# Attention rows scaled when they are written, or when they are gathered

## The chip, the cores and the metric

One core of a Trainium2 chip runs the kernel. The metric is device time in microseconds (us) of one launch, the lower the better. Inputs and outputs are float32 in device memory; a row of 512 floats is 2 KB.

## What is computed

Linear attention with a normalisation, followed by a mixture of eight experts of which each token uses one. Cut to what matters:

```python
kv  = einsum('bhsd,bhse->bhde', k, v)              # 8 batches, 8 heads, 576 tokens, 64 wide
out = einsum('bhsd,bhde->bhse', q, kv)
rms = sqrt(mean(out*out, -1) + 1e-6)               # one number per token and head
x   = (out / rms * g_norm) as [4608 tokens, 512]
logits = x @ w_gate;  e = argmax(logits)           # 8 experts
gate_w = softmax(logits)[e]
eom    = sigmoid(x @ w_output_gate)
y[token] = gate_w * eom[e] * (relu(x @ w1[e]) @ w2[e])
```

Each token thus has eight factors 1/rms (one per head) and one factor gate_w * eom[e], which is called its scale here. The scale is positive, so it may be applied to x in front of the relu or to the result behind w2.

## The kernel before

**First phase.** 4608 tokens are 36 tiles of 128 rows. Eight batches are read in order; for each, `kv_step` (L472) makes kv out of four loads of 512 KB and a remainder, `kvT_part` and `m_part` prepare the products with the gates, and `out_tile` (L540) makes the rows of the tiles whose batches are ready: four or five tiles per batch, one batch behind the loads. ScalarE copies each tile to `xrow` and squares it (`out_rows`), VectorE sums the squares (`sums`, L587).

**Routing.** `route` (L599) is a generator that handles a group of 8, 8, 8, 7 and 5 tiles in eight steps. Step 1 makes `rv` = 1/rms with nine small VectorE instructions (L608 to L622); 2 and 3 make the logits and the one-hot of the expert (`ohb`); 4 counts rows on TensorE (`mrp`, L665 to L672); 5 is two exponentials; 6 makes the scale, multiplies it into `rv` (L701), has GpSimd multiply each tile of the group by `rv` (L710, one instruction per tile, in place) and sends the rows to `xs` in device memory; 7 makes one 128x128 bfloat16 mark matrix per tile (`la`, L720) and the columns `rrc` (L723 to L726); 8 multiplies marks and columns on TensorE (L729) and adds the product to the index table `tsum`. Step 8 of the third group gives the rows of the first run, the lead run: the first 384 tokens of the most frequent expert among the first 24 tiles.

**Order.** PE (TensorE), ACT (ScalarE), DVE (VectorE) and POOL (GpSimd) run their instructions in the order written: a table `STEPS` says after which tile each step of a group is issued, and the string `TAIL` orders what comes behind the last tile. In `TAIL` a digit is the next step of that group, `Q` empties the pending copies and sums, `G` gathers the lead run's rows (`gather(0)`), sets `mark` on POOL (transfers ordered behind the gather wait for it) and opens the late row writes; `W` loads the lead expert's w2; `C` is twelve matmuls of ones into `mrp`; `L` is the next step of the lead run (split of the first w1 block into a high and a low part, three transposed stages, second split, eight `mm1`), and `S` a split of w2. SP (SyncE) issues the plain transfers in program order, each when its semaphores allow.

**Second phase.** Nine runs follow (the lead run, the rest of its expert, seven experts). Per run `mm1` makes eight blocks of h (three matmuls where full precision takes one, since operands are split in two parts; L308), `mm2` makes y tile by tile (L350, L356). During `mm1` of a run the next run's rows are gathered by POOL (L246) as buffers come free; during `mm2` they are transposed (`stage`, L270) and split (L275, L276). `wlo` (L224, L231) is the DVE half of a weight split. y is copied out of PSUM by ACT (L365) and scattered by POOL (L366). A loop behind the runs handles experts with more rows than their capacity; it is not entered in the profile.

The lines around the change, as they stand before:

```python
for j in range(k):                                              # step 6
    xv = x[:, j].rearrange("q (p u d) -> q u p d", p=NP, u=2)
    f = rv[:, c0 + j - g0].rearrange(...).unsqueeze(3).to_broadcast([P, 2, NP, D])
    nc.gpsimd.tensor_tensor(out=xv, in0=xv, in1=f, op=ALU.mult)
xwrite(c0, xs[...], x)
```

## Time and profile before

| | us |
|---|---|
| median of 3 runs | 626.33 |
| lowest, highest | 624.49, 630.56 |
| profiled execution: its time | 623.01 |
| profiled execution: span | 620.9 |
| last tile of the first phase ends on PE | about 124.3 |
| first `mm1` matmul | 158.9 |
| last y tile's matmuls end | about 603.7 |

The profile is of one execution. Busy times overlap between engines; a wait names the engine and line that ended it. PEclk is the clock that TensorE was granted, as a share of 2.4 GHz; 0.5 is its lower level, 1.2 GHz. Times within the span count from its start.

### The profile page before, as it was taken

To read this page: it belongs to the slowest core of one execution; us is meant where nothing else is said; L and a number is where in the kernel's file an instruction comes from. 1 tells how busy PE (TensorE), PEld (TensorE's weight loads), DVE (VectorE), ACT (ScalarE), POOL (GpSimd) and SP (SyncE) were. 2 spreads that over 40 slices of the span, in tenths; PEclk is the share of its full clock that TensorE was granted. 3 is DMA by queue.
4 is the path that set the end of the run, shared out by engine and by line. 5 is a ranking of instruction groups with operands and counts; after the bars stand their busy time and mean duration, and the time that the engine had idled before them with its cause. 6 is when DMAs were issued, how large, how long until landed. Compare 5 with 4: busy or idle time off the path is not lost.

```text
span 620.9 us, 10566 instructions
## 1 busy us (share of the span) xinstructions
PE 571.0 (92%) x4253; PEld 505.7 (81%) x4253; DVE 284.1 (46%) x569; ACT 217.5 (35%) x405; POOL 123.2 (20%) x128
## 2 busy tenths in 40 slices
PE   7895959906899999999999999999999999999995
PEld 5785849804898989988988998799889879988974
DVE  2159698998641445632452144234314523532410
ACT  1364443500632433431343234233414433432310
POOL 1005054163052040041013103200510221011011
PEclk8798675555899999999999999999999999999998
DMA  8999971419246372343233524343343334210001
GB/s 267 357 407 406 408 274 65 142 31 358 69 144 228 113 222 68 104 131 136 70 130 102 167 69 136 120 138 97 116 145 102 109 109 163 69 52 19 1 17 44
DMA packets 28739, 91.64 MB, mean 148 GB/s; under 512 B 4081, under 2 KB 4209, under 8 KB 28688
## 3 DMA queue, kind: packets, MB, share of 16 engines
q1 hardware_dynamic: 21952, 71.33, 32.5%
q0 software_dynamic: 6304, 19.39, 9.9%
q8 instruction: 35, 0.57, 0.4%
q10 hardware_dynamic: 432, 0.21, 0.1%
q14 instruction: 16, 0.13, 0.1%
HBM read 72.03 MB, written 19.41 MB: 147 GB/s over the span
## 4 chain that ended last, share of the span: by engine, by line
PE 80%; DVE 11%; DMA 5%; issue 2%; ACT 1%; POOL 0%; POOLq 0%; ACTq 0%; DVEq 0%
PE hps L308 35%; PE yps L356 31%; PE ops L561 4%; DMA ld<-kvm 3%; DVE la L720 3%; PE yps L350 3%; PE tps L270 3%; PE kvp L487 2%; DMA gcol<-gn 1%; DVE ss L587 1%; PE kvp L503 1%; DVE gp L629 0%; DMA out<-y,oidx 0%; PE mrp L470 0%; ACT sq L577 0%
## 5 line engine op out<-in xcount | busy, mean ns | idle before, releaser
L356 PE MATMUL yps<-whi,hT 128*128 128x512 f32 (+3 forms) x592 | 195.1, 398 | 0.0
L308 PE MATMUL hps<-xT,whi 128*128 128x256 f32 (+8 forms) x1024 | 189.9, 303 | 2.0 <-ACT xT L275 2.0
L308 PEld LDWEIGHTS hps<-xT,whi 128*128 128x128 f32 x1024 | 158.4, 189 | 3.4 <-ACT xT L275 2.2
L356 PEld LDWEIGHTS yps<-whi,hT 128*128 128x128 f32 (+3 forms) x592 | 110.1, 186 | 24.2
L308 PE MATMUL hps<-xT,wlo 128*128 128x304 f32 (+8 forms) x512 | 118.3, 302 | 0.0
L324 DVE SCALAR_TENSOR_TENSOR hT<-hps,hT 128x512 fp32r<-128x512 f32 (+6 forms) x112 | 58.1, 519 | 130.4 <-ACT hT L323 130.4
L356 PE MATMUL yps<-wlo,hT 128*128 128x512 f32 (+3 forms) x296 | 115.9, 392 | 0.0
L323 ACT ACTIVATE hT<-hps 128x512 fp32r<-128x512 f32 (+6 forms) x112 | 51.5, 460 | 141.5 <-PE hps L308 108.6
L308 PEld LDWEIGHTS hps<-xT,wlo 128*128 128x128 f32 x512 | 86.5, 189 | 0.0
L366 POOL DMA_INDIRECT out<-y,oidx x42 | 42.1, 1003 | 215.7 <-ACT y L365 188.9
L246 POOL DMA_INDIRECT xg<-xs,gidx x42 | 41.9, 998 | 169.2 <-PE tps L270 130.3
L356 PEld LDWEIGHTS yps<-wlo,hT 128*128 128x128 f32 (+3 forms) x296 | 55.1, 186 | 11.3
L224 DVE SCALAR_TENSOR_TENSOR wlo<-wraw,gcol,whi 128x1024 fp32r<-128x1024 f32 x32 | 41.1, 1283 | 40.1 <-ACT whi L221 40.0
L710 POOL TENSOR_TENSOR xrow<-xrow,rv 128x512 f32<-128x512 f32 x36 | 36.3, 1044 | 103.6 <-DVE rv L701 64.9
L275 ACT CAST xT<-tps 128x512 fp32r<-128x512 f32 (+9 forms) x45 | 23.1, 518 | 85.0 <-PE tps L270 83.2
L561 PE MATMUL ops<-aug,ld 64*128 64x80 f32 (+1 forms) x640 | 52.5, 331 | 0.0
L276 DVE TENSOR_TENSOR xT<-tps,xT 128x512 fp32r<-128x512 f32 (+9 forms) x45 | 27.1, 606 | 54.8 <-ACT xT L275 50.2
L561 PEld LDWEIGHTS ops<-aug,ld 64*128 64x128 f32 (+1 forms) x640 | 46.4, 232 | 4.0 <-issue 1.8
L365 ACT COPY y<-yps 128x512 f32<-128x512 f32 (+3 forms) x37 | 21.7, 586 | 71.9 <-PE yps L356 68.2
L231 DVE TENSOR_TENSOR wlo<-wraw,whi 128x1024 fp32r<-128x1024 f32 x32 | 39.2, 1225 | 13.7 <-ACT whi L228 8.8
L587 DVE TENSOR_REDUCE ss<-sq 128x8 f32<-128x512 f32 x36 | 24.2, 681 | 30.5 <-ACT sq L577 30.4
L487 PE MATMUL kvp<-ld 128*64 128x64 f32 (+1 forms) x640 | 33.3, 266 | 4.8 <-DMA ld<-kvm 4.5
(155 smaller groups left out, 429.3 us busy)
## 6 DMA issues: line engine op xcount, KB each, us to landing
wraw<-w SPq DMA_DIRECT2D x64, 512.0 KB, 3.4
ld<-kvm SPq DMA_DIRECT2D x32, 512.0 KB, 10.1
ld<-qT SPq DMA_DIRECT2D x18, 512.0 KB, 10.2
xs<-xrow SPq DMA_DIRECT2D x9, 512.0 KB, 4.5
xs<-xrow SPq DMA_DIRECT2D x2, 1280.0 KB, 6.4
xs<-xrow SPq DMA_DIRECT2D x1, 2048.0 KB, 15.3
ld<-rem SPq DMA_DIRECT2D x3, 512.0 KB, 10.1
xg<-xs,gidx POOLq DMA_INDIRECT x42
```

The costliest lines, as they stand in the source:

```text
L224: eng.scalar_tensor_tensor(out=lo, in0=r, scalar=gcol[:, 0:1], in1=hi.bitcast(F32), op0=ALU.mult, op1=ALU.subtract)
L231: eng.tensor_tensor(out=lo, in0=r, in1=hi.bitcast(F32), op=ALU.subtract)
L246: gathered = nc.gpsimd.indirect_dma_start(out=x[:M, :], out_offset=None, in_=rows, in_offset=bass.IndirectOffsetOnAxis(ap=gidx[:M, p, t:t ...
L308: nc.tensor.matmul(ps[:, j, :n], w[:, o:o + P], x[d][:, j * N:j * N + n], start=(d == 0 and k == 0), stop=(d == 3 and k == 2))
L323: nc.scalar.activation(hh, x, AF.Relu)
L324: nc.vector.scalar_tensor_tensor(out=v(h[:, l:l + n]), in0=x, scalar=0.0, in1=hh.bitcast(F32), op0=ALU.max, op1=ALU.subtract)
L356: nc.tensor.matmul(ps[:M], a, b, start=(f == 0 and k == 0), stop=(f == 7 and k == 2))
L366: i_ = nc.gpsimd.indirect_dma_start(out=out, out_offset=bass.IndirectOffsetOnAxis(ap=oidx[:M, p, t:t + 1], axis=0), in_=y[:M], in_offset=N ...
L487: nc.tensor.matmul(ps[u * D:(u + 1) * D, p * D:(p + 1) * D], k, v, start=(s == 0 and p == 0), stop=(s == 4 and p == NP - 1))
L561: nc.tensor.matmul(v[r0:r0 + m, u, p, :], qt[g // 2][r, p, q0:q0 + m], augs[b % 3][r, p, :], start=True, stop=True)
L587: nc.vector.tensor_reduce(out=o, in_=sq, axis=AX.X, op=ALU.add)
L710: nc.gpsimd.tensor_tensor(out=xv, in0=xv, in1=f, op=ALU.mult)
```

## The change

The rows are written to `xs` without any multiplication. A row becomes 528 floats wide (`XW`): 512 values, then the eight factors 1/rms, then the scale, then seven floats of nothing (set to zero at the start). Step 1 of `route` has POOL copy `rv` into the tail of each row buffer (12 small copies in all), step 6 has DVE write the scale there; the multiply by L701 and the 36 POOL multiplies of L710 are gone. Behind each gather, POOL now multiplies the gathered tile by the eight factors of its rows (`scale_heads`, one instruction per gathered tile: 3 in the lead run, 39 in the others); DVE copies the scale to `tl` when the tile is staged; and the scale is applied when y leaves PSUM: as the `scale` of ACT's copy, or, for the five half tiles, with one more DVE instruction. The marks `la` read the float32 tile `ni` where they read a bfloat16 copy of it; they stay bfloat16. `TAIL` is another string: steps 7 and 8 of the fourth group and 2 to 5 of the last stand ahead of the first weight split, two `C` instead of one stand between the last group's steps 4 and 6, the three stages stand ahead of its step 8, and `W` stands behind the second split.

```diff
-TAIL = "Q3G4L434344C4C4C4WCLLLLLLSLSLSLSLLL"
+TAIL = "Q3G4343C44C4CL44CLLL4LWLSLSLSLSLLLL"
...
+NORMS = "PPP"
...
-            x = take([P, DM], F32, "xg")
+            x = take([P, XW], F32, "xg")
...
+    def scale_heads(x, eng):
+        v = x[:, 0:DM].rearrange("p (h d) -> p h d", d=D)
+        f = x[:, C_RMS:C_RMS + H].unsqueeze(2).to_broadcast([x.shape[0], H, D])
+        eng.tensor_tensor(out=v, in0=v, in1=f, op=ALU.mult)
+
+    def scale_rows(i):
+        for k, (t, c0, M) in enumerate(tiles_of(i)):
+            if i == 0 and NORMS[k] == "V":
+                continue
+            scale_heads(xg[(RUNS[i][0], t)][:M], nc.gpsimd)
...
+        tl = cst.tile([P, 1], F32, name="tl", bufs=14)
+        nc.vector.tensor_copy(tl[:M], x[:M, C_SCALE:C_SCALE + 1])
+        tails[(p, t)] = tl
...
+            nc.vector.tensor_scalar(out=y[:M], in0=y[:M], scalar1=tl[:M, 0:1], scalar2=None, op0=ALU.mult)
         else:
-            nc.scalar.copy(y[:M], ps[:M])
+            nc.scalar.activation(y[:M], ps[:M], AF.Copy, scale=tl[:M, 0:1])
...
+        for c0, k, x in chunks_of(gi):
+            nc.gpsimd.tensor_copy(x[:, :, C_RMS:C_RMS + H].rearrange("q t (p u) -> q t u p", u=2),
+                                  rv[:, c0 - g0:c0 - g0 + k].rearrange("q t (u p) -> q t u p", u=2))
...
-        vec.tensor_tensor(out=se[:, :n], in0=se[:, :n], in1=eo[:, :n], op=ALU.mult)
-        vec.tensor_tensor(out=rv, in0=rv, in1=se[:, :n].unsqueeze(2).to_broadcast([P, n, E]), op=ALU.mult)
...
-            for j in range(k):
-                xv = x[:, j].rearrange("q (p u d) -> q u p d", p=NP, u=2)
-                f = rv[:, c0 + j - g0].rearrange("q (u p) -> q u p", u=2).unsqueeze(3).to_broadcast([P, 2, NP, D])
-                nc.gpsimd.tensor_tensor(out=xv, in0=xv, in1=f, op=ALU.mult)
+            t = c0 - g0
+            vec.tensor_tensor(out=x[:, :, C_SCALE], in0=se[:, t:t + k], in1=eo[:, t:t + k], op=ALU.mult)
...
-            vec.tensor_scalar(out=la, in0=nib, scalar1=lon[:, t:t + 1], scalar2=None, op0=ALU.is_equal)
+            vec.tensor_scalar(out=la, in0=ni, scalar1=lon[:, t:t + 1], scalar2=None, op0=ALU.is_equal)
...
             gather(0)
+            scale_rows(0)
             behind.append(nc.gpsimd.memset(mark, 0.0))
...
                 gather(1)
+                scale_rows(1)
...
+                    if f == 3 and not last_run:
+                        scale_rows(i + 1)
```

What this moves, at three places. Names as above; `xg` is a gathered tile, `gp` the logits of a group, `hps` the sums of `mm1`.

POOL, from the first group's rows to the first gather of the second phase, before:

```order
L418 CAST gfull<-cf 128x1728
L710 ISA
L710 TENSOR_TENSOR xrow_125<-xrow_125,rv 128x2x4x64 x8
L710 TENSOR_TENSOR xrow<-xrow,rv 128x2x4x64 x23
L246 DMA xg<-xs,gidx 128x512 x3
L815 MEMSET mark 128x1
L710 TENSOR_TENSOR xrow<-xrow,rv 128x2x4x64 x5
L246 DMA xg<-xs,gidx 128x512 x3
```

and now:

```order
L441 CAST gfull<-cf 128x1728
L646 COPY xrow_123<-rv 128x8x2x4
L646 COPY xrow<-rv 128x2x2x4 x9
L646 COPY xrow<-rv 128x5x2x4
L251 DMA xg<-xs,gidx 128x528 x3
L267 ISA
L267 TENSOR_TENSOR xg<-xg 128x512 x3
L837 MEMSET mark 128x1
L646 COPY xrow<-rv 128x5x2x4
L251 DMA xg<-xs,gidx 128x528 x2
L267 TENSOR_TENSOR xg<-xg 128x512
L251 DMA xg<-xs,gidx 128x528
```

The lead run's gather stood behind 31 multiplies and now stands behind 11 copies; the three multiplies of its tiles stand ahead of `mark` and of the last group's copy.

DVE, from the last group's `rv` (step 1) on, before:

```order
L622 SCALAR_TENSOR_TENSOR rv<-ru,ry 128x40
L223 TENSOR_SCALAR whi<-wraw,gcol 128x1024
L224 SCALAR_TENSOR_TENSOR wlo<-wraw,gcol,whi 128x1024
L629 TENSOR_TENSOR gp<-gp,rv 128x5x64 x2
L720 TENSOR_SCALAR la<-nib,rlon 128x128 x7
L723 TENSOR_TENSOR rrc<-cf,rhk 128x7x48
L725 TENSOR_TENSOR rrc<-rrc,gfull 128x7x48
L726 TENSOR_SCALAR rrc<-rrc,cf 128x7x48
```

and now, a little later in the same stretch (the split's new place):

```order
L658 TENSOR_REDUCE lg<-gp 128x5x8
L703 TENSOR_TENSOR rog<-ohb_119,lg 128x40
L705 TENSOR_REDUCE rogs<-rog 128x5
L706 TENSOR_SCALAR rogs<-rogs 128x5
L228 TENSOR_SCALAR whi<-wraw,gcol 128x1024
L229 SCALAR_TENSOR_TENSOR wlo<-wraw,gcol,whi 128x1024
L713 TENSOR_TENSOR rw<-mrp,ohb_119 128x40
L715 TENSOR_REDUCE slots<-rw 128x5
```

The split of the first w1 block moved from behind step 1 of the last group to just ahead of its step 6 (`rw`).

DVE, up to the split of the lead run's transposed rows (`xT`, six instructions), before:

```order
L906 TENSOR_TENSOR t_142<-tbl,perm 128x336
L874 SCALAR_TENSOR_TENSOR gl<-t_2042 128x6
L908 TENSOR_REDUCE gif<-t_142 128x42
L887 COPY gif<-gl 128x3
L909 CAST gidx<-gif 128x42
L888 CAST gidx<-gif 128x3
L879 TENSOR_SCALAR zf<-gif 128x3
L879 TENSOR_SCALAR zf<-gif 128x42
L880 SCALAR_TENSOR_TENSOR oidx<-gif,zf 128x3
L880 SCALAR_TENSOR_TENSOR oidx<-gif,zf 128x42
L276 TENSOR_TENSOR xT<-tps,xT 128x2x128 x6
```

and now:

```order
L924 TENSOR_TENSOR t_149<-perm,cf 128x56
L297 TENSOR_TENSOR xT<-tps,xT 128x2x128
L925 TENSOR_REDUCE eposf<-t_149 128x7
L926 CAST epos<-eposf 128x7
L297 TENSOR_TENSOR xT<-tps,xT 128x2x128
L287 COPY tl<-xg 128x1
L297 TENSOR_TENSOR xT<-tps,xT 128x2x128 x2
L287 COPY tl<-xg 128x1
L297 TENSOR_TENSOR xT<-tps,xT 128x2x128 x2
L754 TENSOR_TENSOR tsum<-mrp,tsum 128x96
```

The index table's work from `tsum` to `oidx` stood ahead of the six `xT` and now stands behind them.


## Rows read from the trace of the kernel before

**Rows 1.** Stretches of the execution: busy time of PE, of its weight loads, of DVE, ACT and POOL, with counts in brackets; then the granted clock, the share of the DMA engines and GB/s.

```profile
60.00:70.00 10.00, 8.68 (x93) 7.68 (x93) 9.12 (x26) 4.50 (x11) 0.06 (x1) 0.50 1.03 408
70.00:80.00 10.00, 10.00 (x191) 9.06 (x189) 4.22 (x20) 5.20 (x16) 0.00 (x0) 0.80 1.03 405
90.00:100.00 10.00, 10.00 (x118) 8.78 (x116) 8.56 (x27) 3.33 (x10) 0.00 (x0) 0.50 0.08 29
250.00:300.00 50.00, 50.00 (x271) 43.72 (x271) 20.21 (x33) 17.20 (x25) 11.03 (x11) 1.00 0.36 121
```

**Rows 2.** PE in order of time in the first phase: start, time, line, operands, count, and in brackets the idle time before and what ended it. L487 at 39.59, 48.03, 65.48 and 77.58 begins the third, fourth, fifth and sixth batch (counted from 0).

```profile
39.59 0.69 PE L487 MATMUL kvp<-ld 128*64 128x64 f32 x16
...
48.03 0.67 PE L487 MATMUL kvp<-ld 128*64 128x64 f32 x16
...
61.32 0.80 PE L729 MATMUL mrp<-rrc,la 128*128 128x96 bf16 x8 [6.31 <-DVE rrc L726]
...
65.48 1.10 PE L487 MATMUL kvp<-ld 128*64 128x64 f32 x16
...
77.58 0.66 PE L487 MATMUL kvp<-ld 128*64 128x64 f32 x16
...
89.60 0.80 PE L729 MATMUL mrp<-rrc,la 128*128 128x96 bf16 x8 [7.12 <-DVE rrc L726]
...
97.34 0.24 PE L665 MATMUL mrp<-erow,row 128*128 128x72 bf16 x1
```

**Rows 3.** The marks on DVE in order of time: start, time of all, line, count (the first group's, the fourth's, the last's).

```profile
52.38 7.74 DVE L720 TENSOR_SCALAR la<-nib,rlon 128x128 bf16<-128x128 bf16 x8
...
137.76 1.41 DVE L720 TENSOR_SCALAR la<-nib,rlon 128x128 bf16<-128x128 bf16 x7
...
146.45 4.24 DVE L720 TENSOR_SCALAR la<-nib,rlon 128x128 bf16<-128x128 bf16 x5
```

**Rows 4.** POOL's multiplies of rows in order of time (the first group's and the fourth's).

```profile
52.02 8.04 POOL L710 TENSOR_TENSOR xrow<-xrow,rv 128x512 f32<-128x512 f32 x8 [44.60 <-DVE rv L701]
...
127.89 7.07 POOL L710 TENSOR_TENSOR xrow<-xrow,rv 128x512 f32<-128x512 f32 x7 [17.34 <-DVE ra L608]
```

**Rows 5.** Other DVE instructions in order of time: one of the start that takes float32 and a column per partition and gives bfloat16, as the new marks do; the first and the last of the second group's steps 1 to 4 (62.33, 71.45); three sums ahead of the third group's steps 1 to 3 (89.47) and the end of those (97.29).

```profile
7.68 0.28 DVE L425 TENSOR_SCALAR triu<-cf,m 128x128 bf16<-128x128 f32 x1
...
62.33 0.68 DVE L587 TENSOR_REDUCE ss<-sq 128x8 f32<-128x512 f32 x1
...
71.45 0.17 DVE L681 TENSOR_SCALAR rogs<-rogs 128x8 f32<-128x8 f32 x1
...
89.47 1.86 DVE L587 TENSOR_REDUCE ss<-sq 128x8 f32<-128x512 f32 x3
...
97.29 0.23 DVE L652 TENSOR_TENSOR ohb<-rsc,rsx 128x64 bf16<-128x64 f32 x1
```

**Rows 6.** DVE behind the last tile, in order of time: step 6 of the fourth group (126.02); the seven instructions L616 to L622 of step 1 of the last group, first and last (128.10, 134.12); its step 6 (144.78); the index table (153.87 up to the next row); the first `xT`.

```profile
126.02 0.21 DVE L688 TENSOR_TENSOR rw<-mrp,ohb 128x56 f32<-128x56 f32 x1
...
128.10 0.92 DVE L616 SCALAR_TENSOR_TENSOR ru<-ry 128x40 f32<-128x40 f32 x1
...
134.12 0.90 DVE L622 SCALAR_TENSOR_TENSOR rv<-ru,ry 128x40 f32<-128x40 f32 x1
...
144.78 0.20 DVE L688 TENSOR_TENSOR rw<-mrp,ohb 128x40 f32<-128x40 f32 x1 [2.01 <-PE mrp L470]
...
153.87 0.25 DVE L733 TENSOR_TENSOR tsum<-mrp,tsum 128x96 f32<-128x96 f32 x1
...
156.57 0.42 DVE L276 TENSOR_TENSOR xT<-tps,xT 128x256 fp32r<-128x256 f32 x1
```

**Rows 7.** PE in order of time: the matmuls of ones between the phases (12, then 24), the first `mm1` matmuls, and the transposes of the second tile of the run behind the lead run.

```profile
142.01 2.73 PE L470 MATMUL mrp<-ones 128*128 128x256 bf16 x12
146.59 5.28 PE L470 MATMUL mrp<-ones 128*128 128x256 bf16 x24 [1.84 <-DVE cnt L705]
...
158.92 1.20 PE L308 MATMUL hps<-xT,whi 128*128 128x384 f32 x2 [1.96 <-ACT xT L275]
...
182.12 0.60 PE L270 MATMUL tps<-ident,xg 128*128 128x128 f32 x4
```

**Rows 8.** The second phase: POOL's first gather for the run behind the lead run, and its last gather for a later run (order of time); from the chain of work that ended last, the start of that later run's transposes, and the last y tile's scatter from issue to landing.

```profile
173.65 1.72 POOL L246 DMA_INDIRECT xg<-xs,gidx  x1 [22.00 <-PE hps L308]
...
333.95 0.91 POOL L246 DMA_INDIRECT xg<-xs,gidx  x1 [0.58 <-PE tps L270]
...
375.56 0.44 PE tps L270 x4
...
604.55 2.73 DMA out<-y,oidx
```

**Rows 9.** Groups of like instructions: count, busy us, mean ns of one, idle time before: the DVE half of w1's split, and ACT's copy of 1024 columns with a scale (L221) and without (L228).

```profile
L224 DVE SCALAR_TENSOR_TENSOR wlo<-wraw,gcol,whi 128x1024 fp32r<-128x1024 f32 x32 | 41.1, 1283 | 40.1 <-ACT whi L221 40.0
...
L221 ACT ACTIVATE whi<-wraw,gcol 128x1024 fp32r<-128x1024 f32 x31 | 35.7, 1153 | 0.0
L228 ACT CAST whi<-wraw 128x1024 fp32r<-128x1024 f32 x32 | 33.3, 1041 | 0.0
```

**Rows 10.** The last loads of the first phase: SP's last issue of them (start, time, count), and the page's row of these loads (size, median time from issue to landing).

```profile
68.96 1.61 SPq L463 DMA_DIRECT2D ld<-qT  x2
...
ld<-qT SPq DMA_DIRECT2D x18, 512.0 KB, 10.2
```

More of the change, by code (lines that the diff above doesn't have):

```diff
@@ L29 @@
 NT = NTOK // P
+XW = DM + 16
 W = D + 2 * E
+C_RMS = DM
+C_SCALE = DM + H
 CAP = [692, 656, 632, 608, 592, 572, 560, 544]
@@ L237, in drop @@
             give(w)
-    xg, xT, hT = {}, {}, {}
+    xg, tails, xT, hT = {}, {}, {}, {}
     def gather(i):
@@ L262, in stage @@
         x = xg.pop((p, t))
+        if i == 0 and NORMS[k] == "V":
+            scale_heads(x[:M], nc.vector)
         if k == 0:
@@ L340, in mm2 @@
         ny += 1
+        tl = tails.pop((p, t))
         for f in range(8):
@@ L409, in body @@
                                 scalar1=gcol[r, 0:1], scalar2=None, op0=ALU.mult)
-    zrow = c1.tile([P, 4], F32, name="zrow")
+    zrow = c1.tile([XW // 16, 16], F32, name="zrow")
     nc.gpsimd.memset(zrow, 0.0)
-    nc.gpsimd.dma_start(out=xs[0:1, :].rearrange("o (a x) -> (o a) x", x=4), in_=zrow)
+    nc.gpsimd.dma_start(out=xs[0:1, :].rearrange("o (a x) -> (o a) x", x=16), in_=zrow)
     erow = c1.tile([P, E], BF16, name="erow")
@@ L421, in body @@
     tsum = c1.tile([P, 2, E * TMAX], F32, name="tsum")
-    nib = c1.tile([P, P], BF16, name="nib")
-    nc.vector.tensor_copy(nib, ni)
     triu = c1.tile([P, P], BF16, name="triu")
@@ L528, in body @@
             k = NT - sum(BIG.values()) - 2 * ROWS
-            x = c1.tile([P, k, DM], F32, name="xrow0")
+            x = c1.tile([P, k, XW], F32, name="xrow0")
         elif g in BIG:
             k = BIG[g]
-            x = mem.tile([P, k, DM], F32, name="xrow", tag=f"xT{list(BIG).index(g)}")
+            x = mem.tile([P, k, XW], F32, name="xrow", tag=f"xT{list(BIG).index(g)}")
         else:
             k = 2
-            x = take([P, k, DM], F32, "xrow")
+            x = take([P, k, XW], F32, "xrow")
         chunks.append((g, k, x))
+        nc.gpsimd.memset(x[:, :, C_SCALE:XW], 0.0)
         g += k
@@ L574, in out_rows @@
         v = ps[:, :, 0:NP * W].rearrange("q u (p y) -> q u p y", p=NP)
-        nc.scalar.copy(xrow.rearrange("q (p u d) -> q u p d", p=NP, u=2), v[:, :, :, 0:D])
+        nc.scalar.copy(xrow[:, 0:DM].rearrange("q (p u d) -> q u p d", p=NP, u=2), v[:, :, :, 0:D])
         sq = wk.tile([P, H, D], F32, name="sq", bufs=4)
@@ L1069, in body @@
                     ws.append(t)
-            x = so.tile([P, DM], F32, name="ox")
+            x = so.tile([P, XW], F32, name="ox")
             nc.gpsimd.indirect_dma_start(out=x, out_offset=None, in_=xs,
                                          in_offset=bass.IndirectOffsetOnAxis(ap=gi[:, 0:1], axis=0))
+            scale_heads(x, nc.gpsimd)
             ps = pt.tile([P, 4, P], F32, name="ops")
@@ L1089, in body @@
             y = so.tile([P, DM], F32, name="oy")
-            nc.scalar.copy(y, py)
+            nc.scalar.activation(y, py, AF.Copy, scale=x[:, C_SCALE:C_SCALE + 1])
             nc.gpsimd.indirect_dma_start(out=out, out_offset=bass.IndirectOffsetOnAxis(ap=oi[:, 0:1], axis=0),
@@ L1109, in build @@
     out = nc.dram_tensor("out", (NTOK, DM), F32, kind="ExternalOutput").ap()
-    xs = nc.dram_tensor("xs", (NTOK + 1, DM), F32).ap()
+    xs = nc.dram_tensor("xs", (NTOK + 1, XW), F32).ap()
     tab = nc.dram_tensor("tab", (P, NOVER), F32).ap()
```

## The prediction

> **What bounds the kernel now.** I read the stretches first, then PE in order of time, then the engines that PE waits for.
>
> From 158.92 on PE is never short of work: busy 50.00 of 50 us at full clock in a stretch like 250 to 300, with DVE at 20.2 and ACT at 17.2 [rows 1], and the transfers hidden. What comes before 158.92 can be shortened; what comes after is 462.0 us of the 620.9 and moves only if it is disturbed.
>
> In the first phase PE stands twice for the same thing: 6.31 us before 61.32 and 7.12 us before 89.60, both until DVE has the columns `rrc` of step 7 [rows 2]. In front of `rrc` stand the marks: 7.74 us for eight, about 0.96 each, where the fourth group's seven took 1.41 us, 0.20 each [rows 3]. Those of 0.96 ran beside POOL's multiplies (52.02 to 60.06, about 1.0 each), those of 0.20 after the fourth group's had ended at 134.96 [rows 4]. So each mark waited for one POOL instruction. It is the same with the seven small instructions 128.10 to 134.12: about 1.0 us apart, again beside seven multiplies [rows 4, 6].
>
> Each stop costs twice: the clock is 0.50 in 60 to 70, behind the first stop, and still 0.50 in 90 to 100 with PE busy throughout, behind the second [rows 1].
>
> The Trainium skill ("SBUF — State Buffer", section "SBUF: two separate sides") says that DVE and GpSimd share one pair of ports, held exclusively for a whole instruction, and that a DVE instruction in a two-port mode, or one with two inputs from SBUF, has to wait. The trace agrees: 0.96 us against 0.20.
>
> **Term 1, the first phase: 17.8 us less.** The multiplies leave this phase; what POOL gets is 12 copies of 16 to 64 columns, at most one marks' pitch (0.20) each for DVE and off PE's path. The new marks read float32. The nearest row is `triu`, float32 to bfloat16 with a column operand, 0.28 us [rows 5]; bounds 0.20 and 0.28 a mark; I take 0.20, the pitch, so eight take 1.6.
>
> - First stop: the marks end at 54.0, `rrc` adds 1.3, PE goes on at 55.3 and not at 61.32: 6.0. It has then waited about 0.3 us, and I keep its clock. The piece to the fifth batch took 4.2 us at half clock (61.32 to 65.48); at full some 2.5, which sets the batch's start to 57.8.
> - Fifth batch: the third, of as many tiles, took 8.4 us at full clock (39.59 to 48.03 [rows 2]); with 0.3 for the matmuls of step 4 it ends at 66.5, not at 77.58.
> - Sixth batch up to the second group's marks: 4.9 us (77.58 to the stop, 89.60 less 7.12 [rows 2]), so PE asks for `rrc` at 71.4. DVE: steps 1 to 4 with their sums take 9.3 us without a pause (62.33 to 71.6 [rows 5]); from 56.0 that is 65.3. Then three sums and step 6, 3.5 together, marks 1.6, `rrc` 1.2: 71.6. Both arrive together, and PE goes on at 71.8, not at 89.60: **17.8**.
> - Behind this DVE is late. From 89.47 to the end of the one-hot at 97.52 it took 8.05 us without a multiply beside it [rows 5]: now 71.7 to 79.8. PE at full clock needs about 4.3 us for what it took 7.7 for at half clock (89.60 to 97.34 [rows 2]), is there at 76.1, and stands 3.7 us.
>
> That stand decides the size. Stops of 6.3 and 7.1 took the clock away, and behind the second it did not return while the phase lasted. I take it that 3.7 us does the same. From 79.8 on all then runs as it ran from 97.5: PE at half clock, DVE level with it, 17.8 us earlier to the end. DVE's step 6 of the fourth group starts at S = 108.2 instead of 126.02.
>
> **Term 2, from S to the first `mm1`: 8.5 us less.** It took 158.92 - 126.02 = 32.9. Now, from S, by DVE's own pieces without a multiply beside them: step 6 of the fourth group 1.65, step 1 of the last 2.2 (it took 7.3 with the seven held ones [rows 6]), marks and columns 2.15, steps 2 and 3 2.6, step 4 1.1: S + 9.7. The first split (2.0) stands here now: S + 11.7. Step 6 of the last group waits for ones, as at 144.78 [rows 6], but for two `C` behind step 4 instead of one. PE starts the first `C` at S + 7.2 (2.7 us), counts rows, and needs 5.3 us for 24 ones at half clock [rows 7]: S + 15.7. Step 6 1.7, five marks 1.0 (they took 4.2 [rows 3]), columns and the expert order 2.6: first `xT` at S + 20.7. The index table's 2.7 us (153.87 to 156.57 [rows 6]) now stands behind the `xT`. From the first `xT` to `mm1` it took 2.35; three `tl` copies add about 0.4. `mm1` starts at S + 23.4: 9.5 less. If the ones warm PE earlier, 24 cost 1.5 to 2 us less.
>
> Against that I set 1.0 us. The lead run's gather no longer waits behind 31 multiplies, and its three tiles are multiplied shortly before S, beside DVE's two-input instructions of the fourth group. Bounds: 0, and 3.1 (all three multiplies). The rows are ready some 15 us ahead of their transposes.
>
> **Term 3, the second phase: 0.5 us more.** POOL gets 39 multiplies of about 1.0 us. For late runs they have cover: the last gather of a run is issued at 333.95, its transposes begin at 375.56 [rows 8]. Not so for the run behind the lead run: its first gather is issued 14.7 us after `mm1` starts (173.65), its second tile transposed at 23.2 (182.12 [rows 7, 8]). In these 8.5 us POOL now has four gathers (1.72, and three of 0.91 with a gap of 0.3: 5.4 in all), two multiplies (2.1) and what is left of the first tile's landing (2.7 from issue to landing, as the last scatter's [rows 8], so up to 1.7): 7.5 to 9.2. Bounds 0 and 2 us late; I take 0.5. DVE's extra work (42 copies `tl`, five short multiplies of half tiles) falls where DVE is 40% busy; without that cover it would be some 9 us at the marks' 0.20 each. ACT's copy with a scale costs 0.11 us more per 1024 columns [rows 9]; only the last one lies on the path. w2's loads move behind the last row write on SP; they land 1 to 3 us ahead of their splits by my count, bounds 0 and 3 us lost.
>
> **Sum.** 623.0 (the profiled execution's time, 2.1 over its span) - 17.8 - 8.5 + 0.5 = 597.2. The median shown, 626.33, lies 3.3 above that execution, its lowest run 1.5. **I predict 597 us.**
>
> **Rivals.**
>
> *The clock survives the 3.7 us.* Then DVE is the bound from 79.8: seventh batch with step 6, marks and table of the third group to 90.6, then sums and steps 1 to 6 of the fourth, S near 102 instead of 108.2: **591**. For it: PE is dense around that stand, and 70 to 80 shows 0.80 after a stop [rows 1], so the clock does come back in this phase. Against: behind the second stop it did not.
>
> *The clock falls at the first, short wait and stays low.* Then only the two stops go, 13.1 us, and the work that ran at full clock between them (in 70 to 80, and up to 82.5; some 8 us) takes about 7 longer: 6 us instead of 17.8, **609**. Against: a wait of 0.3 us is short.
>
> *The marks take long of themselves*, and the change to float32 doesn't shorten them: then the stops stay and only the seven small instructions and the order of the tail are gained, about 5 us: **618**. Against: 0.20 each without POOL [rows 3].
>
> *Slower: the multiplies bite in the loop.* By the port rule each of the 39 can hold a DVE weight split of 1.28 us, one of two inputs from SBUF [rows 9], or be held by it, and DVE's later halves of h wait behind. On POOL a multiply that waits for its gather to land stands in front of the scatters and of the next gather. It decides once rows or splits arrive later than PE's slack. If each multiply cost PE its full 1.04 us, 40.6 us come back: **638**. Against: 42 us of cover for a later run, DVE at 40%. For: the cover of the run behind the lead run is about used up. The Trainium skill's rule, named above, allows this; by it alone the sum would go up by no more than these 40.6.
>
> *Loads as the bound of the first phase*: the last are issued by 70.6 and land near 80.8 [rows 10]; the last batch's products and five tiles need some 7 us more, about 88 in all. S at 102 or 108 lies behind that, so I give this no chance of its own.
>
> **How the numbers follow.** Forecast 0.50, clock kept 0.28, clock low early 0.13, long marks 0.05, slower 0.04. The forecast's own range is 592 to 604: the collisions (0 to 3), the next run's rows (0 to 2), w2 (0 to 3), warm ones (-2), and the 1.5 to 3.3 us by which the shown runs lie above the profiled one. To hold 8 in 10 the range takes in the kept clock and the early low one: 586 to 612. One per cent, 6.3 us, is about what can be told from no change. Below 620 lie the first three and part of the fourth: faster 0.93, same 0.03, slower 0.04.
>
> **What would show it.** The profile of the changed kernel should have marks of 0.2 to 0.28 us each in all groups; no wait of PE for `rrc` over 1 us; one wait of 3 to 4 us for `ohb` near 76 to 80; the clock at 0.50 behind it (if at 1.00, the first rival); step 6 of the fourth group near 108; 23 to 25 us from there to `mm1`; `mm1` starting near 132; and from there 462 to 464 us to the end. If that last stretch has grown by more than 3 us, the fourth rival is at work; if PE still stands 6 us at marks, the third. I am wrong in kind if DVE or POOL is what PE waits for in the second phase.

## The result, and the profile after

The changed kernel takes **596.42 us** in the median (589.71 to 596.93, 4 runs) beside 625.64 of the kernel before: ratio 0.949, 95% interval 0.941 to 0.958. The profiled execution took 596.93 us, its span is 595.1. Executions over 1.5% slower than the fastest of their kernel (up to 1426 us, with matmuls about twice as long in that one) are left out of the ratios, but two of the profiles below, of "before, no multiplies" and of "30 + 90 ones", are of such executions.

All comparisons below use four marks of an execution. T is the start of the fourth batch (batches are counted from 0, as in the prediction), ahead of the first group's marks; S is DVE's step 6 of the fourth group; M is the first `mm1` matmul; the end is that of the span. T differs from one execution to the next, without the change (47.65 to 51.69, and 61.64 once) as with it (45.69 to 51.79).

| profiled execution of | T | T to S | S to M | M to end | span |
|---|---|---|---|---|---|
| before | 48.03 | 78.0 | 32.9 | 462.0 | 620.9 |
| the change | 51.73 | 60.3 | 21.0 | 462.0 | 595.1 |

PE of the changed kernel in order of time (start, time, line, operands, count, in brackets the idle time before and what ended it):

```profile
51.73 0.67 PE L508 MATMUL kvp<-ld 128*64 128x64 f32 x16
...
58.75 0.50 PE L750 MATMUL mrp<-rrc,la 128*128 128x96 bf16 x8
61.07 0.66 PE L508 MATMUL kvp<-ld 128*64 128x64 f32 x16
...
75.35 0.50 PE L750 MATMUL mrp<-rrc,la 128*128 128x96 bf16 x8 [1.00 <-DVE rrc L747]
...
83.31 0.35 PE L695 MATMUL mrp<-ohb,ones 128*128 128x64 bf16 x8 [3.37 <-DVE ohb L677]
...
84.96 2.00 PE L583 MATMUL ops<-aug,ld 64*128 64x80 f32 x16
...
122.32 3.99 PE L491 MATMUL mrp<-ones 128*128 128x256 bf16 x24
...
133.08 1.02 PE L329 MATMUL hps<-xT,whi 128*128 128x384 f32 x2 [2.42 <-ACT xT L296]
```

The two stops of 6.31 and 7.12 us [rows 2] are gone: no wait at 58.75, 1.00 us before 75.35. The one stand left is the 3.37 us for the one-hot; behind it a tile's sixteen matmuls take 2.00 us, where they took 1.12 ahead of it. DVE shows why the stops went, and the collision near S (same columns):

```profile
55.88 1.65 DVE L741 TENSOR_SCALAR la<-ni,rlon 128x128 bf16<-128x128 f32 x8
...
72.55 1.65 DVE L741 TENSOR_SCALAR la<-ni,rlon 128x128 bf16<-128x128 f32 x8
...
109.33 0.87 DVE L706 TENSOR_SCALAR rogs<-rogs 128x7 f32<-128x7 f32 x1
110.12 2.02 DVE L609 TENSOR_REDUCE ss<-sq 128x8 f32<-128x512 f32 x3
112.06 0.21 DVE L713 TENSOR_TENSOR rw<-mrp,ohb 128x56 f32<-128x56 f32 x1
...
112.55 0.55 DVE L717 TENSOR_SCALAR rhk<-slots 128x7 f32<-128x7 f32 x1
```

Eight marks take 1.65 us instead of 7.74 [rows 3]. Beside POOL's three multiplies for the lead run `rogs` and `rhk` are stretched (0.87 and 0.55; both take 0.17 elsewhere). The stretches of the changed kernel (busy time of PE, its loads, DVE, ACT, POOL; then the granted clock, DMA share, GB/s):

```profile
10.00:20.00 10.00, 7.79 (x85) 5.11 (x81) 0.50 (x2) 0.96 (x3) 0.00 (x0) 0.61 1.03 350
20.00:30.00 10.00, 10.00 (x116) 9.21 (x118) 1.37 (x2) 3.02 (x7) 0.00 (x0) 0.50 1.02 393
30.00:40.00 10.00, 10.00 (x172) 8.87 (x170) 2.74 (x4) 5.87 (x14) 0.00 (x0) 0.70 1.03 418
...
80.00:90.00 10.00, 6.70 (x83) 6.12 (x84) 8.93 (x39) 3.39 (x11) 1.18 (x4) 0.69 0.69 250
90.00:100.00 10.00, 9.56 (x112) 8.38 (x113) 4.01 (x16) 3.62 (x10) 0.00 (x0) 0.50 0.88 310
100.00:110.00 10.00, 9.20 (x104) 8.49 (x102) 9.17 (x29) 6.69 (x16) 4.51 (x6) 0.50 0.23 59
```

and of the kernel before, for the start:

```profile
10.00:20.00 10.00, 7.85 (x109) 5.43 (x107) 0.50 (x2) 0.96 (x3) 0.00 (x0) 0.84 1.04 336
20.00:30.00 10.00, 9.76 (x140) 8.72 (x137) 1.52 (x3) 4.55 (x13) 0.00 (x0) 0.69 1.01 345
30.00:40.00 10.00, 9.35 (x206) 8.38 (x208) 3.60 (x6) 7.47 (x21) 0.00 (x0) 1.00 1.03 408
```

The clock of the first 40 us differs from execution to execution (0.84, 0.69, 1.00 before; 0.61, 0.50, 0.70 here). From 20 to 40 PE is never idle here, so this clock is what makes T 3.7 us later. Behind the 3.37 us stand it is 0.69 in 80 to 90 and 0.50 from 90 to 110.

In the second phase PE's waits are 0.3 us for a multiply, once, and the start of `mm1` itself (waiting engine and line, what ended it: us in total, times, longest):

```profile
PE hps L329 <- ACT xT L296: 2.4, 1, 2.4
PE tps L291 <- POOL xg L267: 0.3, 1, 0.3
```

That M to end is 462.0 in both does not mean that nothing changed in it. In the first 5 us of `mm1` the granted clock is 1.00 here and was 0.66 before, so the transposes of the run behind the lead run begin 19.4 us behind M instead of 20.7. From there to the end it takes 442.6 us instead of 441.3. PE, before (one row) and now (its second tile shows the wait):

```profile
179.60 0.60 PE L270 MATMUL tps<-ident,xg 128*128 128x128 f32 x4
```

```profile
152.47 0.60 PE L291 MATMUL tps<-ident,xg 128*128 128x128 f32 x4
...
155.50 0.66 PE L291 MATMUL tps<-ident,xg 128*128 128x128 f32 x4 [0.35 <-POOL xg L267]
```

### The profile page after: what moved, and what is told of

Read it like the earlier page. It is cut to its first block, busy times and chain, and to the rows that moved or that the text cites. A ratio compares the mean times of both kernels' runs of the same rounds, so it can differ in the third digit from the quotient of the medians.

```text
span 595.1 us, 10650 instructions
## 1 busy us (share of the span) xinstructions
PE 564.3 (95%) x4253; PEld 499.8 (84%) x4253; DVE 264.9 (45%) x617; ACT 221.1 (37%) x405; POOL 139.0 (23%) x158
## 4 chain that ended last, share of the span: by engine, by line
PE 83%; DVE 8%; DMA 3%; issue 2%; ACT 2%; POOL 1%; SPq 0%; POOLq 0%; DVEq 0%; ACTq 0%
PE hps L329 34%; PE yps L378 32%; PE ops L583 5%; PE kvp L508 3%; PE yps L372 3%; PE tps L291 3%; DMA ld<-rem 2%; PE mrp L491 2%; DVE ss L609 1%; PE kvp L524 1%; DMA xg<-xs,gidx 1%; DVE gp L654 1%; DVE la L741 1%; DVE lg L658 1%; PE mrp L534 0%
## 5 line engine op out<-in xcount | busy, mean ns | idle before, releaser
L389 POOL DMA_INDIRECT out<-y,oidx x42 | 43.9, 1044 | 144.3 <-ACT y L388 103.1
L378 PEld LDWEIGHTS yps<-wlo,hT 128*128 128x128 f32 (+3 forms) x296 | 55.1, 186 | 11.2
L229 DVE SCALAR_TENSOR_TENSOR wlo<-wraw,gcol,whi 128x1024 fp32r<-128x1024 f32 x32 | 43.6, 1362 | 39.9 <-ACT whi L226 39.7
L267 POOL TENSOR_TENSOR xg<-xg 128x512 f32<-128x512 f32 (+8 forms) x42 | 45.6, 1087 | 43.6 <-DMA xg<-xs,gidx 35.9
L388 ACT ACTIVATE y<-yps,tl 128x512 f32<-128x512 f32 (+3 forms) x37 | 25.5, 689 | 71.6 <-PE yps L378 68.5
L583 PE MATMUL ops<-aug,ld 64*128 64x80 f32 (+1 forms) x640 | 50.6, 326 | 0.0
L583 PEld LDWEIGHTS ops<-aug,ld 64*128 64x128 f32 (+1 forms) x640 | 44.6, 226 | 3.9 <-issue 1.7
L226 ACT ACTIVATE whi<-wraw,gcol 128x1024 fp32r<-128x1024 f32 x31 | 35.5, 1145 | 0.0
```

Source lines behind the costliest of these rows:

```text
L226: he.activation(hi, r, AF.Copy, scale=gcol[:, 0:1])
L229: eng.scalar_tensor_tensor(out=lo, in0=r, scalar=gcol[:, 0:1], in1=hi.bitcast(F32), op0=ALU.mult, op1=ALU.subtract)
L267: eng.tensor_tensor(out=v, in0=v, in1=f, op=ALU.mult)
L378: nc.tensor.matmul(ps[:M], a, b, start=(f == 0 and k == 0), stop=(f == 7 and k == 2))
L389: i_ = nc.gpsimd.indirect_dma_start(out=out, out_offset=bass.IndirectOffsetOnAxis(ap=oidx[:M, p, t:t + 1], axis=0), in_=y[:M], in_offset=N ...
L583: nc.tensor.matmul(v[r0:r0 + m, u, p, :], qt[g // 2][r, p, q0:q0 + m], augs[b % 3][r, p, :], start=True, stop=True)
```

## The experiments

The marks T, S, M of each profiled execution; the text under it says what each kernel is.

| kernel | T | T to S | S to M | M to end | span | ratio to before, interval |
|---|---|---|---|---|---|---|
| before + float32 marks | 47.65 | 79.9 | 34.4 | 461.5 | 623.4 | 1.002 (0.999 to 1.005) |
| before, no multiplies | 61.64 | 74.4 | 25.4 | 461.6 | 623.0 | 0.957 (0.950 to 0.963) |
| before + new order | 48.61 | 77.8 | 29.4 | 462.4 | 618.2 | |
| before + ones at the stops | 51.69 | 71.9 | 34.4 | 461.5 | 619.5 | 0.991 (0.988 to 0.995) |
| change, old order | 45.69 | 57.6 | 23.9 | 463.6 | 590.8 | 0.959 (0.952 to 0.965) |
| change, step 4 later | 46.01 | 57.2 | 21.2 | 463.1 | 587.5 | 0.946 (0.940 to 0.951) |
| change + 30 ones | 46.47 | 53.6 | 21.5 | 462.4 | 583.9 | 0.939 (0.934 to 0.943) |
| 30 ones, no multiplies | 51.48 | 53.6 | 18.9 | 462.2 | 586.1 | 0.938 (0.933 to 0.943) |
| 30 ones, lead run on ACT | 51.79 | 53.6 | 18.9 | 464.3 | 588.6 | 0.943 (0.939 to 0.948) |
| 30 + 90 ones | 51.64 | 54.2 | 20.8 | 462.9 | 589.5 | 0.939 (0.930 to 0.947) |
| 30 ones + ones at the start | 49.84 | 54.2 | 19.2 | 463.7 | 586.9 | 0.940 (0.935 to 0.944) |

**Float32 marks alone.** In the kernel before:

```diff
-            vec.tensor_scalar(out=la, in0=nib, scalar1=lon[:, t:t + 1], scalar2=None, op0=ALU.is_equal)
+            vec.tensor_scalar(out=la, in0=ni, scalar1=lon[:, t:t + 1], scalar2=None, op0=ALU.is_equal)
```

> The kernel before with one edit: the marks read the float32 tile ni; the 36 multiplies on GpSimd stay. Theory (a mark is long because it waits for a GpSimd multiply, whatever the type of its input): the first group's eight marks still take 7 to 8 us, TensorE still stands 6 to 7 us twice, 623 to 628 us. Rival (marks that read bfloat16 are held and marks that read float32 are not): eight marks take 1.6 to 2.2 us, both stops go, 606 to 612 us.

Measured: no change (622.57 to 627.11 us). The first group's marks and PE's first stop, each in order of time:

```profile
52.00 7.77 DVE L720 TENSOR_SCALAR la<-ni,rlon 128x128 bf16<-128x128 f32 x8
```

```profile
60.98 0.80 PE L729 MATMUL mrp<-rrc,la 128*128 128x96 bf16 x8 [6.34 <-DVE rrc L726]
```

So the type of the marks' input is not what makes them long; whether the multiplies beside them are, the next kernel shows. One thing expected was missed: the second stop is 4.91 us, not 6 to 7. PE came to it later, as its clock was 0.50 from 60 to 80 in this execution.

**The multiplies taken out.** The kernel before without the loop of L710, all else as it was:

```diff
-            for j in range(k):
...
-                nc.gpsimd.tensor_tensor(out=xv, in0=xv, in1=f, op=ALU.mult)
             xwrite(c0, xs[1 + c0 * P:1 + (c0 + k) * P].rearrange("(t p) x -> p t x", p=P), x)
```

> The kernel before without the 36 multiplies on GpSimd (the rows stay without their factors 1/rms and scale); its order string and bfloat16 marks stay. Theory (the multiplies are what held DVE): eight marks take 1.6 us, TensorE stands under 1.5 us for the columns, first phase and tail as in the changed kernel with the old order, the second phase 461 to 462 us: 598 to 602 us. Rival (the gathered multiplies of the changed kernel cost something in the second phase): then this kernel is 2 us or more below the changed kernel with the old order. Second rival (something else in the step holds DVE): 620 us or more.

Three of its five runs took 594.90 to 600.59 us. The profiled one took 624.85, and tells two things. The marks, bfloat16 here, take 1.38 us for eight, and PE does not wait for `rrc` in the first three groups:

```profile
66.01 1.38 DVE L716 TENSOR_SCALAR la<-nib,rlon 128x128 bf16<-128x128 bf16 x8
...
68.23 0.31 DVE L722 TENSOR_SCALAR rrc<-rrc,cf 128x384 bf16<-128x384 bf16 x1
```

```profile
73.93 0.82 PE L725 MATMUL mrp<-rrc,la 128*128 128x96 bf16 x8
...
99.60 0.51 PE L725 MATMUL mrp<-rrc,la 128*128 128x96 bf16 x8
...
122.31 0.82 PE L725 MATMUL mrp<-rrc,la 128*128 128x96 bf16 x8
```

At the clock it had, PE came late to the first, so DVE's side is the better measure there: `rrc` is ready 6.9 us behind T, where it was ready 13.2 behind it before. At full clock PE asked for it 7.0 behind T (61.32 less 6.31, T 48.03 [rows 2]).

And PE's clock stayed at its lower level though the profile shows no pause of PE (columns as above):

```profile
30.00:95.00 65.00, 65.00 (x797) 58.38 (x795) 30.43 (x95) 29.66 (x76) 0.00 (x0) 0.50 0.94 355
```

That put T at 61.64; T to S, 74.4, has the low clock in it too and can't be compared. S to M is 25.4 with the old order and no multiply beside it, 7.5 less than before: here the seven small instructions, and the last group's marks, wait for nothing.

**The order alone, both ways.** The changed kernel with the old string, and the kernel before with the new one:

```diff
-TAIL = "Q3G4343C44C4CL44CLLL4LWLSLSLSLSLLLL"
+TAIL = "Q3G4L434344C4C4C4WCLLLLLLSLSLSLSLLL"
```

> The changed kernel with the order string of the kernel before. Theory (most of what the stretch from step 6 of the fourth group to the first mm1 lost came from the multiplies leaving DVE alone: 5.1 us of small instructions and 3.2 us of marks): step 6 of the fourth group starts where it does in the changed kernel, 111 to 113, the stretch takes 24 to 26 us instead of 21.0, and the time is 599 to 602 us. Rival (the order is what shortened it): the stretch takes 29 to 33 us, 604 to 609 us.

> The kernel before with the order string of the changed kernel and nothing else. Theory (the order is worth what the changed kernel lost with the old string, 2.9 us, since it moves the index table and a split off the path): step 6 of the fourth group to first mm1 29 to 31 us instead of 32.9, 621 to 624 us. Rival (with GpSimd's multiplies still there the lead run's gather is late, and the new order gains nothing): 32 to 34 us, 624 to 627 us.

S to M is 23.9 with the old string (21.0 with the new) in the changed kernel, 29.4 with the new (32.9 with the old) in the kernel before: the order is worth 2.9 to 3.5 us, multiplies or not. (With all multiplies and the old order, S to M is 32.9 in one profile and 34.4 in two others below, so in the kernel before it may be worth up to 5.0.) Two of the four runs of the kernel before with the new string took 619.75 and 620.20 us, a little under the 621 to 624 expected; the other two lie far off.

The changed kernel with the old string took 592.57 and 596.10 us in two of its four runs, below the 599 to 602 expected, since its first phase was shorter than in the changed kernel's own profile. The string does not touch that phase, so this is a second look at it: here T is at 45.69, the stand for the one-hot is again 3.37 us, but the clock came back some 9 us behind it (the sixteen matmuls of a tile take 1.12 us again), and T to S is 2.8 us shorter:

```profile
77.26 0.42 PE L695 MATMUL mrp<-ohb,ones 128*128 128x64 bf16 x8 [3.37 <-DVE ohb L677]
...
86.77 1.12 PE L583 MATMUL ops<-aug,ld 64*128 64x80 f32 x16
```

**Ones where PE stood, in the changed kernel.** They write columns that nothing reads:

```diff
+FILL = (2, 30)
...
         prev = list(ohsum)
+        if gi == FILL[0]:
+            constant(mrp[:, 256:512], FILL[1])
```

> The changed kernel with 30 matmuls of ones on TensorE ahead of step 4 of the third group, where it stood 3.4 us for the one-hot; nothing waits for them. Theory (the stand is what took the clock): granted clock 1.0 from 80 to 100, DVE then the bound, step 6 of the fourth group at 103 to 106 instead of 112.06, 587 to 592 us. Rival (the clock falls there whatever TensorE does, or small matmuls don't hold it): clock 0.5 in 90 to 110 as in the changed kernel, 596 to 598 us.

Measured: 585.71 us (584.72 to 588.90), T to S 53.6 instead of 60.3. The total is below the 587 to 592 expected because T was 5.3 us earlier than in the changed kernel's profile. PE in order of time, then a stretch:

```profile
74.42 3.45 PE L492 MATMUL mrp<-ones 128*128 128x256 bf16 x30
...
78.03 0.35 PE L698 MATMUL mrp<-ohb,ones 128*128 128x64 bf16 x8
```

```profile
80.00:90.00 10.00, 9.08 (x188) 7.99 (x188) 9.46 (x43) 6.79 (x20) 0.00 (x0) 1.00 1.06 382
```

PE's matmuls with the one-hot come as late as before (31.6 us behind T in both); only the clock is different, 1.00 instead of 0.69, and DVE, at 9.46 of 10 us, is the bound. The 6.7 us are thus the price of the clock behind the 3.37 us stand in the changed kernel's profile; beside the old-order profile, in which the clock came back, it is 4.0. The four runs of this version lie below all four of the changed kernel, but not by the ones alone: of the 11.2 us between the two profiled spans, 5.3 are T.

**The same in the kernel before**, all multiplies left in place: 50 ones ahead of step 8 of groups one and two, 30 ahead of step 4 of the third.

> The kernel before, all multiplies left where they were, with matmuls of ones where TensorE stands: 50 ahead of step 8 of the first and of the second group, 30 ahead of step 4 of the third; nothing waits for them. Theory (a stop costs its own length and then the clock behind it): both stops stay some 6 us long (ones and wait together), the granted clock is 1.0 from 60 to 75 and behind the second stop, the second stop ends near 84 instead of 89.6, step 6 of the fourth group starts near 118 to 121, 612 to 619 us. Rival (the stop's own length is all that counts, DVE sets the rest): 622 to 627 us.

The clock is 1.00 in all stretches from 60 to 100, and T to S 71.9 instead of 78.0, though the stops stay (ones and wait together; the second, then one stretch):

```profile
80.50 5.63 PE L472 MATMUL mrp<-ones 128*128 128x256 bf16 x50
87.70 0.50 PE L735 MATMUL mrp<-rrc,la 128*128 128x96 bf16 x8 [1.57 <-DVE rrc L730]
```

```profile
80.00:90.00 10.00, 8.43 (x113) 7.41 (x110) 9.90 (x17) 2.06 (x6) 6.51 (x7) 1.00 0.87 332
```

The second stop ends 36.0 us behind T, as against 41.6 before (89.60 less 48.03 [rows 2]): that is the 84 expected, once the 3.7 us by which T is later are taken off. The total was missed: 620.99 us in the median, not 612 to 619, and the ratio of 0.991 is under the one per cent that can be told. T is 3.7 us later and S to M 1.5 us longer in this profile. Of the 17.7 us that T to S lost by the change, then, some 6 can be had by the clock alone; the rest needs the marks to be short.

**Step 4 later, no ones.** The order could perhaps do what the ones do:

```diff
-         {25: 1, 26: 2, 27: 1, 28: 1, 29: 1, 30: 1, 31: 1},
+         {25: 1, 26: 2, 28: 2, 29: 1, 30: 1, 31: 1},
```

> The changed kernel with step 4 of the third group issued one tile later (with its step 5), no ones added. Theory (any work in that place keeps the clock, and the order alone can supply it): TensorE runs the last batch's first matmuls and a tile where it stood, the stand for the one-hot falls from 3.4 us to under 1.5 us, the clock stays at 1.0 to 90, step 6 of the fourth group 53.5 to 55 us behind the fifth batch's start instead of 60.3, 586 to 592 us. Rival (the stand only moves, or steps that come later make DVE late): 60 us or more behind it, 595 to 598 us.

The total (590.96 us in the median) lies in the expected range, in the profiled execution only because T was 5.7 us earlier than in the changed kernel's. The stand shrank to 1.47 us, but the clock fell behind it all the same, and T to S is 57.2, not 53.5 to 55:

```profile
77.57 0.35 PE L695 MATMUL mrp<-ohb,ones 128*128 128x64 bf16 x8 [1.47 <-DVE ohb L677]
...
78.95 2.00 PE L583 MATMUL ops<-aug,ld 64*128 64x80 f32 x16
```

```profile
80.00:90.00 10.00, 9.56 (x106) 8.38 (x105) 6.39 (x34) 3.88 (x10) 0.00 (x0) 0.50 1.06 383
```

Beside the 1.57 us above, behind which the clock stayed at 1.00, the length of the stand alone does not tell whether it falls; what does was not settled.

**No multiplies of gathered tiles.** From here on the changed kernel with the 30 ones is the base. All calls of `scale_rows` are left out:

```diff
             gather(0)
-            scale_rows(0)
...
                 gather(1)
-                scale_rows(1)
...
-                    if f == 3 and not last_run:
-                        scale_rows(i + 1)
```

> The changed kernel with the 30 ones, without any of the 42 multiplies of gathered tiles (the rows keep no 1/rms; the scale is still applied). Theory (the lead run's three multiplies hold DVE about 2.7 us around step 6 of the fourth group, the other 39 cost at most 0.5 us): step 6 of the fourth group to first mm1 18.5 to 19.5 us instead of 21.5, second phase 461.5 to 462.5, 582 to 584 us beside 585.7 with them. Rival (the multiplies delay the second phase too): its stretch from mm1 on is 2 us or more shorter than with them, 578 to 581 us.

S to M is 18.9 instead of 21.5, M to end 462.2 instead of 462.4. The three multiplies of the lead run thus cost 2.6 us in that execution. It depends on what they meet: in the profile with ones at the start (below) only `rogs` and `rhk` are held, and T to M is 0.9 us longer than without multiplies (73.4 to 72.5), where with the 30 ones alone it is 2.6 longer (75.1).

The 39 multiplies of the second phase cost 0.2 us in this pair of profiles. Other profiles put them at about 1: from the first transposes of the run behind the lead run to the end it takes 441.4 to 442.9 us in the seven with them, 440.7 to 441.7 in the six without. The total (587.0 us in the median) was not the 582 to 584 expected: T alone is 5.0 us later than in the kernel with them.

**The lead run's multiplies on ACT**, 24 instructions of 64 columns with a scale per partition, instead of three on POOL:

```diff
+            if i == 0 and NORMS[k] == "A":
+                x = xg[(RUNS[i][0], t)]
+                for h in range(H):
+                    v = x[:M, h * D:(h + 1) * D]
+                    nc.scalar.activation(v, v, AF.Copy, scale=x[:M, C_RMS + h:C_RMS + h + 1])
```

> The changed kernel with the 30 ones and the lead run's three tiles multiplied on ACT, eight small instructions each, instead of on GpSimd. Theory (GpSimd's multiply is what holds DVE, ACT's instruction does not): no DVE instruction of 0.9 us or more among the small ones near step 6 of the fourth group, mm1 2 to 3 us earlier, 582 to 584 us. Rival (ACT is then late with the exponentials or the copies of the last group): 585 to 589 us.

First DVE with the 30 ones and POOL's multiplies, then ACT and DVE with ACT's, in order of time:

```profile
100.75 1.07 DVE L723 SCALAR_TENSOR_TENSOR rlon<-rhk,slots 128x7 f32<-128x7 f32 x1
...
102.28 0.95 DVE L734 TENSOR_TENSOR xrow<-rdn 128x2 f32<-128x2 f32 x2
...
103.58 1.05 DVE L639 SCALAR_TENSOR_TENSOR ru<-ry 128x40 f32<-128x40 f32 x1
```

```profile
104.81 5.82 ACT L277 ACTIVATE xg<-xg 128x64 f32<-128x64 f32 x24
```

```profile
106.08 0.17 DVE L730 SCALAR_TENSOR_TENSOR rlon<-rhk,slots 128x7 f32<-128x7 f32 x1
...
106.71 0.24 DVE L741 TENSOR_TENSOR xrow<-rdn 128x2 f32<-128x2 f32 x2
...
107.29 0.20 DVE L646 SCALAR_TENSOR_TENSOR ru<-ry 128x40 f32<-128x40 f32 x1
```

DVE is not held by ACT at all, and S to M falls by the same 2.6 us. It did not become time: 589.95 us in the median, not the 582 to 584 expected. T is 5.3 us later than in the kernel with POOL's multiplies, and M to end is 464.3, with the run behind the lead run now waiting for its rows, as the third term feared:

```profile
147.08 0.66 PE L299 MATMUL tps<-ident,xg 128*128 128x128 f32 x4 [1.73 <-POOL xg L269]
```

The Trainium skill ("SBUF — State Buffer", section "SBUF: two separate sides") says that on the side of the engines only the port pair that DVE and GpSimd share makes them wait, and that ACT waits for nobody. The trace agrees for DVE: `rlon` takes 0.17 us beside ACT's 24 instructions, 1.07 beside POOL's.

**More ones**: 30 also ahead of the fourth group's step 4 and 60 ahead of its step 8.

> The changed kernel with the 30 ones and, likewise, 30 ahead of step 4 of the fourth group and 60 ahead of its step 8 (where TensorE stands 3.7 and 10.3 us). Theory (DVE is the bound from 90 on, TensorE's clock matters there only for what DVE waits for): the last tile's matmuls and the ones take half as long, first mm1 blocks run at full clock, 1 to 3 us off: 583 to 585 us. Rival (no effect, DVE alone sets the end): 585 to 586.5 us; or the 60 run at half clock and end behind rrc: 587 to 590 us.

The 60 took 9.10 us at the lower clock and were themselves what `rrc`'s matmuls came behind; T to S 54.2, S to M 20.8, the four runs 582.29 to 591.25 us: no gain, as the rival had it.

**Ones at the start.** Two kernels fill the gaps of the first batch, in which PE waits for loads: one with the lead run on ACT (its profile is of the execution of 1426 us and not used), one without. Their expectations count batches from one; their "fifth" is T's.

```diff
-COLD = (2, 20, 2, 3, 3, 12)
+COLD = (7, 15, 4, 4, 4, 12)
```

> The changed kernel with the 30 ones, the lead run's tiles multiplied on ACT, and more matmuls of ones in the first batch, where TensorE waits for loads (7 instead of 2 ahead of each piece, 4 instead of 2 and 3 later in that batch). Theory (the execution's loss before the fifth batch is the clock, which falls in the gaps of the first batch): granted clock 1.0 in 10 to 40, fifth batch begins at 45.5 to 47 in the profiled execution instead of 51.7, 582 to 585 us and the runs within 3 us of each other. Rival (the clock falls between 13 and 20 whatever TensorE does): fifth batch at 51 to 52, 587 to 591 us. Second rival (the loads bound the phase): fifth batch earlier, the end not.

> The changed kernel with the 30 ones ahead of step 4 of the third group, the lead run's multiplies on GpSimd again, and more matmuls of ones in the first batch where TensorE waits for loads (7 instead of 2 ahead of each piece, 4 instead of 2 and 3 later in it). Theory (what differs between executions up to the fifth batch is the clock, which falls in the gaps of the first batch): clock 1.0 in 10 to 40, fifth batch begins at 45.5 to 47 in the profiled execution, 582 to 585 us. Rival (the clock falls between 13 and 20 all the same): fifth batch at 51 to 52, 586 to 590 us. Second rival (loads or DVE make up for an early start): fifth batch at 45.5 to 47, but step 6 of the fourth group not below 100, 585 to 587 us.

The second took 586.08 to 588.70 us, no better than the kernel with the 30 ones alone (584.72 to 588.90). The first took 585.32 to 587.94, some 3 us below the kernel with the lead run on ACT (586.89 to 590.41); without a profile to compare, why stays open. Neither came to the 582 to 585 expected. In the second the clock now holds in 10 to 20 (1.00, where it was 0.61 in the changed kernel) but falls later:

```profile
10.00:20.00 10.00, 7.57 (x120) 5.80 (x120) 0.50 (x2) 1.46 (x5) 0.00 (x0) 1.00 1.03 348
20.00:30.00 10.00, 8.08 (x110) 6.94 (x106) 1.78 (x3) 4.15 (x11) 0.00 (x0) 0.75 1.02 377
30.00:40.00 10.00, 10.00 (x178) 8.97 (x177) 2.46 (x5) 5.75 (x14) 0.00 (x0) 0.74 1.03 418
```

T is at 49.84, between the two values expected. The ones moved the fall to the next gaps; whether ones there too would keep T at 46 was not tried.

## Why the prediction was right, and where it was not

The total came out (597 predicted, 596.42 in the median, 596.93 profiled), but by luck in part, because two misses cancelled: the first term was to give 17.8 and gave 14.0 at S, the second was to give 8.5 and gave 11.9; the third was to cost 0.5 and added nothing to M to end. Had T been at 48.03 again, the profiled execution would have taken about 593 us (an estimate: 596.93 less 3.7), nearer to the first rival's 591.

**Term 1.** Its mechanism and size hold from T on: 78.0 to 60.3 us is 17.7 less, for 17.8 predicted. So do its steps, 3.7 us later each: PE's first stop was to end at 55.3 (58.75 less 3.7 is 55.1), the second at 71.8 (75.35), the one-hot to be met at 79.8 after a stand of 3.7 (83.31 after 3.37), the clock to be 0.50 behind it (it is). What failed is a step that stands in it only silently: the kernel up to T was taken over from one execution, as if its clock would repeat. T was between 45.69 and 51.79 in twelve profiles, and 61.64 in one. A term made against one execution's own start carries that spread; it was in the range only as the few us by which runs differ.

**The choice of the cause.** That marks wait for multiplies was inferred from 0.96 and 0.20 us. It is now shown from both sides: float32 marks beside multiplies take 7.77 us, bfloat16 marks without them 1.38. The price per mark was right (0.20; the bfloat16 ones take 0.17 in the kernel without multiplies, so the new type costs at most 0.3 us per eight).

**The stand decides the size.** The ones show it: with them in its place T to S falls by 6.7 us, for 6.2 that the first rival allowed (S at 102 instead of 108.2). That it always loses the clock for the rest of the phase was too strong: the old-order kernel's profile has the same stand and the clock back within it. Its span, 590.8, less the 2.9 us that the order is worth, makes an estimate of 587.9; the changed kernel's run of 589.71 has a span of 587.8. It may thus have been such a case (with T early too: that estimate has T at 45.69), but it was not profiled.

**Term 2.** S + 23.4 predicted, S + 21.0 measured. The 24 ones were the term that was mis-sized: 5.3 us at half clock were taken, they took 3.99, since the clock rose under them (the text had put a warm PE at 1.5 to 2 us less); step 6 came at S + 14.3, not 15.7. From there to the first `xT` 4.3 us for 5.0 (whose own pieces, 1.7, 1.0 and 2.6, add up to 5.3), and 2.4 for 2.75 to `mm1`. The order's own share, which the prediction never separated, is 2.9 to 3.5 us; the multiplies' leaving is most of the rest (7.5 by the kernel without them). The collision of the lead run's multiplies was priced at 1.0 between 0 and 3.1: `rogs` and `rhk` lost 0.70 and 0.38 in the profile of the change (`rogs` ahead of S, so that its part lies in T to S), and 2.6 us were lost in another execution, where each of the three multiplies met a two-input instruction.

**Term 3 and the slower rival.** 462.0 us before and after, but by a second cancelling: the clock at the start of `mm1` gave 1.3 us, and from the next run's transposes on 1.3 us were lost, where the term had 0.5 between 0 and 2. About half of it is lost at the place that was named, the run behind the lead run: from its first transposes to those of the run after it 32.1 us instead of 31.4, with 0.35 us of PE waiting for the second tile's rows. With another timing this wait was 0.7 (second tile) and 1.73 us (first tile). DVE's w1 split did grow, 1362 ns in the mean for 1283 [rows 9], and it is 1284 again without multiplies; ACT's copy of y takes 689 ns for 586. PE shows no wait for either. The rival at 638 falls with the kernel that has no multiplies (462.2).

**The other rivals.** Marks long of themselves: excluded. A low clock early: not by a short wait, as that rival had it (at 58.75 there was none, and behind the 1.00 us at 75.35 a tile took 1.12), but at the start of the execution, and the profile without multiplies (T at 61.64) shows what it can cost.

## What to carry to other kernels

When GpSimd works on SBUF tiles beside many small DVE instructions, count DVE's waits by GpSimd's instruction time, not by DVE's own, and move that work to where DVE has slack, or to ACT: 36 multiplies cost over 20 us in one place, 39 of the same kind about 1 us in another. A stop of TensorE is to be priced twice, by its length and by the clock behind it; matmuls of ones in the stop show the second price in one run and may be kept there, though more of them in other places gained nothing here. And compare profiles from a mark behind the start, since executions of one program differ there by more than many changes are worth.
